# A given TensorE order, fixed loads, longer filler products and a last product by halves in a fused retention and two-product kernel

## The chip, the cores and the metric

The kernel runs on one core of one Trainium2 chip. The metric is the device time of one execution in microseconds (us), lower is better. Times are medians of several executions. Ratios are the mean time of one kernel's fast runs over that of the other's fast runs of the same rounds, so they are not quite the ratios of the medians quoted beside them. A run is called slow if it is over 1.5% above the fastest run of the same kernel. I also group runs by the mean clock that TensorE was granted, which every run records.

## The reference, cut to what matters

```python
# q, k, v: (8, 8, 576, 64) f32;  w_in: (512, 2048);  w_out: (2048, 512)
scores = scale * np.matmul(q, k.transpose(0, 1, 3, 2))
Dmat = np.where(rel >= 0, gamma[:, None, None] ** rel[None, :, :], 0.0)   # decay per head, causal
attn = np.matmul(scores * Dmat[None], v)
x = attn.transpose(0, 2, 1, 3).reshape(4608, 512)
h = x @ w_in              # the "first product"
g = h * np.cos(h)
return g @ w_out          # the "second product"
```

## The kernel before

The attention is done in chunks of 64 tokens, in "sessions" of short 64x64 products (q by k, state, q by state, p by v). They yield x for one of nine blocks of 512 tokens. Each block then goes through the first product (`mlp1`, four matmuls of 512 or, in the early blocks, 256 columns per tile), ACT's sine for the cosine, DVE's multiplication, and the second product. From the second block on, the second product is computed by seven half-size products in place of eight (`wino2`).

The kernel is written as a list of tasks, and a scheduler in Python decides at build time the order of every engine's instructions. Before, that scheduler is greedy. It also keeps an account of TensorE's instructions:

```python
def fetched(t):        # earliest start of task t, by TensorE's instruction count
    k, s = math.ceil(count / 256 - 1.754), 0
    while k >= 0 and (k + 1.754) * 256 <= count + t.ni + (self.MARGIN if t.ni > 60 else 0):
        if k < len(got):
            s = max(s, got[k] - t.dur * ((k + 1.754) * 256 - count) / t.ni)
        elif t.ni > 60:
            s = max(s, free["pe"] + self.FETCH - t.dur)      # FETCH = 6000 ns
        k += 1
    return s
```

`count` is the number of instructions placed so far, a task of many short products (`ni` over 60) isn't started shortly before a border of 256 instructions, and each border assumes that the next one can't be passed within 6 us. I shall call this the guard.

At the start, filler products run on TensorE while data arrives (181 of 128 columns, 14.3 us in all), and the eight slabs of the weight matrices (0.5 MB each, issued from POOL) wait for two events:

```python
inst = e.matmul(ap(self.at(self.wb), 512, 0, 128, 0, [1, 128]), self.ONE.ap(), self.ONE.ap(), ...)   # filler, 128 columns
...
gate = [(self.kv[1, 0, 0]["stgq"],)]                     # q of the second stream
for s, x in enumerate((0, 2, 1, 3)):
    self.load_w("win", x, gate if s >= self.LEAD else [(self.kv[0, 0, 0]["stgv"], 0)], 100 + s)
for s in range(4):
    self.load_w("wout", s, gate, 200 + s)
```

The "second stream" is the second pair of the four sequences of the batch with which the kernel starts; the cast of the second half of its v (`natv`) stands on POOL too.

## Time and profile before

| | before |
|---|---|
| median of the runs before the prediction | 308.38 us (305.6 to 308.73, 3 runs) |
| its profiled run | 312.0 us, span 310.3, clock 0.994, slow |
| TensorE busy | 294.1 us of 310.3 |
| DVE, ACT, POOL busy | 66%, 61%, 35% |

TensorE is the bound and the rest is slack, so the question is where TensorE stands still. The prediction below shows the views that carry this. Two more sets of lines are wanted later for comparison: the queue that brings instructions (packets, MB, share of 16 engines' span), and two windows (columns: stretch, length, then busy us of PE, PEld, which is TensorE's weight loads, DVE, ACT and POOL, each with its number of instructions, then clock, DMA share, GB/s).

```profile
q8 instruction: 34, 0.56, 0.8%
```

### The profile page before, as it was taken

The page shows a single profiled execution, that of the slowest core. Times are in us where ns is not written, and L with a number is a line of the kernel's source. Part 1 is how long each engine was busy: PE and PEld are TensorE (multiplying, and loading weights), DVE is VectorE, ACT ScalarE, POOL GpSimd, SP SyncE. Part 2 cuts the span into 40 slices and gives each one's busy share as a digit, 9 for nine tenths or more (in the row PEclk, how much of TensorE's full clock was granted, in tenths as well). Part 3 has the DMA queues.
Part 4 walks back from the last instruction along what each step waited for, and adds up shares of the span by engine and source line. Part 5 has one row for each costly group of instructions (what it writes and reads, how often), then busy time and mean ns, then how long its engine had stood idle before and what let it go on. Part 6 is the DMA issues. An engine that isn't in the chain of part 4 may idle for free.

```text
span 310.3 us, 10091 instructions
## 1 busy us (share of the span) xinstructions
PE 294.1 (95%) x4274; PEld 214.7 (69%) x4277; DVE 206.3 (66%) x371; ACT 188.3 (61%) x340; POOL 108.9 (35%) x134
## 2 busy tenths in 40 slices
PE   8987999799889999999998799999999999999995
PEld 8866755688778888567855375768656666666684
DVE  3574973475984769898478487775769667666641
ACT  3476843888959775856373566474686665455430
POOL 2261058759517581931362631312741000000000
PEclk9999999999999999999999799999999999999999
DMA  9999999999977999894999749269701100300123
GB/s 172 222 159 206 205 229 217 253 270 219 219 157 189 122 204 285 159 171 109 234 219 247 181 48 235 61 114 195 161 13 72 70 2 0 127 10 2 63 76 136
DMA packets 126397, 46.80 MB, mean 151 GB/s; under 512 B 105104, under 2 KB 122000, under 8 KB 126352
## 3 DMA queue, kind: packets, MB, share of 16 engines
q1 hardware_dynamic: 122128, 41.95, 63.3%
q0 software_dynamic: 4224, 4.19, 8.4%
q8 instruction: 34, 0.56, 0.8%
q14 instruction: 11, 0.09, 0.1%
HBM read 36.70 MB, written 9.44 MB: 149 GB/s over the span
## 4 chain that ended last, share of the span: by engine, by line
PE 87%; DVE 3%; ACT 3%; issue 2%; DMA 2%; POOL 2%; DVEq 0%
PE bk L763 39%; PE bk L886 32%; PE bk L800 4%; PE bk L418 2%; DMA stgq<-in_q_dram 2%; PE bk L661 2%; PE bk L652 2%; PE bk L634 2%; PE st L643 2%; PE bk L575 2%; DVE gt L774 1%; PE bk L593 1%; DVE pt L723 1%; POOL win L743 1%; POOL wout L747 1%
## 5 line engine op out<-in xcount | busy, mean ns | idle before, releaser
L774 DVE TENSOR_TENSOR gt<-bk,cb 128x256 bf16<-128x256 f32 (+1 forms) x192 | 103.7, 555 | 59.5 <-ACT cb L771 52.9
L763 PE MATMUL bk<-xt,win 128*128 128x256 bf16 (+1 forms) x768 | 140.1, 327 | 2.3 <-issue 1.3
L771 ACT ACTIVATE cb<-bk,cpi 128x256 bf16<-128x256 f32 (+1 forms) x192 | 108.4, 585 | 55.6 <-PE bk L763 54.0
L763 PEld LDWEIGHTS bk<-xt,win 128*128 128x128 bf16 x768 | 72.9, 98 | 44.0 <-issue 2.3
L512 POOL TENSOR_TENSOR natv<-stgv,wv 128x512 bf16<-128x512 f32 x38 | 41.3, 1097 | 36.1 <-DMA stgv<-in_v_dram 23.3
L477 POOL CAST natk<-stgk 128x512 bf16<-128x512 f32 x36 | 22.0, 626 | 62.0 <-DMA stgk<-in_k_dram 34.6
L557 POOL TENSOR_TENSOR qnat<-stgq,wq 128x512 bf16<-128x512 f32 x36 | 38.6, 1092 | 13.5 <-DMA stgq<-in_q_dram 5.9
L723 DVE TENSOR_TENSOR pt<-bk,tri 128x512 bf16<-128x512 f32 (+1 forms) x46 | 29.6, 683 | 14.8 <-PE st L643 12.8
L476 ACT ACTIVATE sbd<-st 128x512 bf16<-128x512 f32 x32 | 19.3, 603 | 22.6 <-PE st L643 22.4
L886 PE MATMUL bk<-wout,s 128*128 128x256 bf16 x256 | 32.2, 273 | 0.0
L886 PE MATMUL bk<-tw,s 128*128 128x256 bf16 x256 | 31.6, 273 | 0.5 <-DVE s L847 0.5
L886 PE MATMUL bk<-wout,gt 128*128 128x256 bf16 x256 | 31.6, 273 | 0.0
L886 PEld LDWEIGHTS bk<-wout,s 128*128 128x128 bf16 x256 | 24.7, 98 | 6.6
L886 PEld LDWEIGHTS bk<-tw,s 128*128 128x128 bf16 x256 | 24.6, 98 | 6.1 <-DVE s L847 0.8
L886 PEld LDWEIGHTS bk<-wout,gt 128*128 128x128 bf16 x256 | 24.7, 98 | 4.6 <-DVE pt L723 0.2
L476 ACT ACTIVATE sn<-bk 128x512 f32<-128x512 f32 x24 | 14.4, 604 | 18.7 <-PE bk L886 18.7
L476 ACT ACTIVATE xt<-bk 128x512 bf16<-128x512 f32 x36 | 23.1, 694 | 0.3 <-PE bk L661 0.2
L898 DVE TENSOR_TENSOR os<-bk,sn 128x512 f32<-128x512 f32 x24 | 16.4, 685 | 8.2 <-PE bk L886 8.2
L886 PE MATMUL bk<-tw,gt 128*128 128x256 bf16 x128 | 17.3, 282 | 0.0
L886 PEld LDWEIGHTS bk<-tw,gt 128*128 128x128 bf16 x128 | 12.9, 101 | 4.2 <-issue 0.6
L418 PE MATMUL bk<-one 128*128 128x128 bf16 x181 | 14.3, 244 | 1.1 <-DVE lq L441 1.1
L800 PE MATMUL bk<-wout,gt 128*128 128x512 bf16 x61 | 14.8, 379 | 0.2
(63 smaller groups left out, 230.7 us busy)
## 6 DMA issues: line engine op xcount, KB each, us to landing
stgk<-in_k_dram SPq DMA_DIRECT2D x32, 256.0 KB, 5.0
stgv<-in_v_dram SPq DMA_DIRECT2D x32, 256.0 KB, 5.4
out_dram<-os SPq DMA_DIRECT2D x15, 512.0 KB, 3.5
stgq<-in_q_dram SPq DMA_DIRECT2D x12, 512.0 KB, 7.0
stgq<-in_q_dram SPq DMA_DIRECT2D x8, 256.0 KB, 4.9
win<-in_moe_w_in_dram POOLq DMA_DIRECT2D x4, 512.0 KB, 7.6
wout<-in_moe_w_out_dram POOLq DMA_DIRECT2D x4, 512.0 KB, 14.7
out_dram<-os SPq DMA_DIRECT2D x6, 256.0 KB, 3.5
```

What stands on the lines that cost most here:

```text
L418: inst = e.matmul(ap(self.at(self.wb), 512, 0, 128, 0, [1, 128]), self.ONE.ap(), self.ONE.ap(), start=True, stop=True, skip_group_check=True)
L476: return self.one(eng, dur, lambda e: e.activation(dst(), src(), AF.Copy), r=r, w=w, **kw)
L477: return self.one(eng, dur, lambda e: e.tensor_copy(dst(), src()), r=r, w=w, port=True, **kw)
L512: self.one(ve, vd, lambda e, b2=b2: e.tensor_tensor(ap(self.at(t["natv"]), 1024, 0, 128, 512 * b2, [D, H], [1, D]), ap(self.at(t["stgv"]), ...
L557: self.one("dve" if fast else "pool", 620 if fast else 990, lambda e, t=t, y=y: e.tensor_tensor(ap(self.at(t["qnat"]), 1024, 0, 128, y * 5 ...
L723: self.one("dve", 610, lambda e, hp=hp: e.tensor_tensor(ap(self.at(pt), 1024, p0, n, 512 * hp, [64, 8], [1, 64]), ap(self.at(sc[hp]), 512, ...
L763: inst = e.matmul(ap(self.at(bk), 512, 0, 128, 0, [1, n]), ap(self.WIN, 4 * DFF, 0, 128, c * DFF + 128 * f, [1, 128]), ap(self.at(xt), 204 ...
L771: self.one("act", 70 + n, lambda e: e.activation(ap(self.at(cb), TB, 0, 128, 0, [1, n]), ap(self.at(bk), 512, 0, 128, 0, [1, n]), AF.Sin, ...
L774: self.one("dve", 75 + n / 0.96, lambda e: e.tensor_tensor(ap(self.at(gt), NF * TB, 0, 128, f * TB + 256 * h0, [1, n]), ap(self.at(bk), 51 ...
L800: inst = e.matmul(self.at(bk).ap(), ap(self.at(gt), NF * TB, 0, 128, f * TB + 256 * half + 128 * tt, [1, 128]), ap(self.WOUT, NF * DM, 0, ...
L886: inst = e.matmul(ap(self.at(bank), 512, 0, 128, 256 * tt, [1, 256]), l(f, tt), rr(f), start=(first and f == 0 and tt == 0), stop=True, sk ...
L898: self.one("dve", 610, lambda e: e.tensor_tensor(view(h, c), ap(self.at(bank), 512, 0, 128, 0, [256, 2], [1, 256]), ap(self.at(sn[name]), ...
```

## The change

The intent is to take the last idle time off TensorE: a literal order of TensorE's 412 tasks, found offline, in place of the greedy choice and of the guard; loads in a fixed order; the weight slabs released at three points; fewer and longer filler products; the last product by token halves so that the last copies and stores overlap. The diff also brings a part that its few words don't name: the first product of the last two token blocks by seven products. The core of it, with cuts marked:

```diff
-            deps += [d for d in readers if d.eng != eng or d.sem or sem]
+            deps += [d for d in readers if d.eng != "pe" or eng != "pe"]
...
-        def fetched(t):
-            ... (the guard, and its use when a task is picked)
...
+                if e == "pe" and t.idx != first or e == "sp" and lead and t is not lead[0]:
+                    continue
...
+    SEVEN = 7
+    ORDER = [int(x) for x in """3 2 0 1 9 4 5 7 6 10 8 11 16 20 14 15 12 13 34 21 ... 409 411 410""".split()]
+    FIRST = [(0, "v", 0), (1, "q", 0), (1, "v", 0)]
...
-                inst = e.matmul(ap(self.at(self.wb), 512, 0, 128, 0, [1, 128]), self.ONE.ap(), self.ONE.ap(),
+                inst = e.matmul(self.at(self.wb).ap(), self.ONE.ap(), ap(self.ONE, 128, 0, 128, 0, [0, 4], [1, 128]),
...
+        for s, x in enumerate((0, 2, 1, 3, 4, 5, 6, 7)):
+            x1, n, b2 = self.FIRST[min(s, len(self.FIRST) - 1)]
+            t = self.kv[x1, 0, 0]
+            gate = [(t["stgq", b2],) if n == "q" else (t["stg" + n], b2)]
+            self.load_w("win" if s < 4 else "wout", x % 4, gate, 100 + s)
...
+            if not last and j + 1 >= self.SEVEN:
+                self.xsums(j + 1)
+                for g in range(4):
+                    self.mlp1w(j + 1, g, base + PER * g / 4, PER / 4)      # seven products, 256 columns
...
+                    for f in range(8) if final else range(4 * q, 4 * q + 4):
+                        for tt in (q,) if final else range(2):             # last product: one token half after the other
```

## The prediction

> **What bounds the kernel now.** I read the page first (busy shares and slices), then ten-microsecond windows, then what TensorE waited for, then the chain that ended last.
>
> ```profile
> PE 294.1 (95%) x4274; PEld 214.7 (69%) x4277; DVE 206.3 (66%) x371; ACT 188.3 (61%) x340; POOL 108.9 (35%) x134
> PE   8987999799889999999998799999999999999995
> PEclk9999999999999999999999799999999999999999
> ```
>
> TensorE is the bound: 95% busy, no other engine over 66%. The clock row has one dip, beside a dip of PE. The windows say where the missing 5% lies:
>
> ```profile
> 20.00:30.00 10.00, 6.83 (x139) 5.54 (x140) 6.66 (x14) 6.04 (x13) 4.36 (x6) 1.00 1.20 196
> 50.00:60.00 10.00, 8.12 (x165) 5.19 (x165) 5.48 (x6) 6.00 (x11) 7.61 (x9) 1.00 1.27 241
> 80.00:90.00 10.00, 8.24 (x150) 6.98 (x148) 9.80 (x19) 6.90 (x14) 2.71 (x3) 1.00 1.13 226
> 170.00:180.00 10.00, 7.25 (x67) 4.11 (x68) 4.66 (x7) 5.43 (x9) 6.88 (x7) 0.83 0.64 162
> 250.00:260.00 10.00, 10.00 (x158) 6.90 (x157) 6.58 (x11) 6.13 (x10) 0.00 (x0) 1.00 0.01 2
> 300.00:310.30 10.30, 7.05 (x65) 6.08 (x63) 1.38 (x2) 1.79 (x3) 0.00 (x0) 0.99 0.29 104
> ```
>
> Columns: PE, PEld, DVE, ACT and POOL busy, clock, DMA share, GB/s. Idle PE: 3.2 us in the third window, 1.9, 1.8 and 2.8 in the next three, and 3.2 at the end. The row at 250 is typical of the rest: PE full, everything else with room. Before 20 us PE looks busy but is mostly filler products. What TensorE waited for, then the chain:
>
> ```profile
> PE st L643 <- issue: 3.3, 1, 3.3
> PE bk L634 <- POOL natv L512: 1.8, 1, 1.8
> PE bk L763 <- issue: 1.3, 1, 1.3
> ```
>
> ```profile
> 18.07 2.30 POOL win L743 x3
> 20.36 2.22 POOL wout L747 x3
> 22.59 1.08 POOL natv L512
> ...
> 26.40 2.07 PE bk L763 x18
> 28.47 1.30 issue
> ...
> 165.96 0.86 PE bk L763 x4
> ...
> 169.47 3.28 issue
> ...
> 173.22 1.55 PE bk L763 x4
> ...
> 307.09 0.60 ACT os L476
> ```
>
> Two things to see. The session of the second stream at 23.8 us waited for a cast that stood on POOL behind six weight issues. And twice TensorE stopped for "issue". One L763 tile is four products, so 18 is not a whole number of tiles: no semaphore stands at that place, and the same holds for the other stop, which fell 29 products into a group of 32. I read both as missing instructions. After the second, four 512-column products took 1.55 us instead of 0.86.
>
> [...] Here 8551 PE and PEld instructions make 33.4 blocks, and the instruction queue moved 34 packets of 0.56 MB together[...]. [...] after 3.28 us the rate was 388 ns a product against 215. [...] DMA share is over 1.0 in all windows up to 90 us, at only 160 to 250 GB/s.
>
> **The change part by part.** Most of the diff rewrites the scheduler; what reaches the chip is this.
>
> (a) Not in the change's short title: the first product of the last two token blocks becomes seven products instead of eight (the scheme that the second product has already). One block now costs 64 products of 512 columns, at 0.86/4 = 215 ns: 13.8 us. New: 4 groups x 7 x 4 = 112 products of 256 columns, at 0.87/8 = 109 ns (chain rows of eight): 12.2 us. Gain 1.6 us a block, 3.2 for two, all on TensorE, which is full there. Costs on other engines, per block: ACT +12 copies x 603 ns = 7.2 us; DVE 12 additions x 685 = 8.2 and four sums at some 0.45 us (estimate: half of the 0.78 us row, plus overhead) = 1.8, minus 12 multiplications x 689 = 8.3 that go to POOL, so +1.7; POOL 12 x about 1.1 us (its natv row) = 13.2. Once: eight weight sums on DVE, six at about 0.75 and two in place at 1.49 (the rows of the sums it makes already) = 7.5 us. With PE's 24.4 us a period, ACT comes to 16 x 0.69 + 12 x 0.60 + 2.4 = 20.6 us, DVE to about 21. Both below PE, but at 85%. The accumulating bank is handed to ACT or DVE four times per group; [...] two groups or other products must interleave, as the given order does. I count 2.2 us of the 3.2.
>
> (b) Start. Six of the eight slabs now wait for the second stream's v instead of its q. v was issued from 12.2 to 16.8 us and lands 5 to 6.6 us after each issue starts, so by about 20; its cast began at 22.56. With at most two slabs ahead of it, up to 2.5 us. Fillers shrink from 181 of 128 columns to about 57 of 512 (14.3 us of filler[...]): some 250 instructions, one block, fewer before the stop at 28.5 us, worth up to 1.3. Against it: block 0 has only 13.9 + 13.8 us of products, and the next stream's data is bound by DMA. So of 3.8 I keep 2.
>
> (c) The given order. It interleaves the second batch of sessions with block 0's second product and puts x-side first products between y-side sessions, which should fill most of the 1.9 us at 50 to 60; and it may fill the 1.8 at 80 to 90, where DVE is 98% busy. Keep 2.2 of 3.7.
>
> (d) The long stop: 3.28 idle plus 1.8 at half clock (0.69 for the first four products, 0.84 for the next eight, 0.26 for twelve more) = 5.1 us. It belongs to the profiled run, 312.0 us; the timed runs are 305.6, 308.4 and 308.7, so only part is in their median. Nothing in the new scheduler models instruction fetch, but the order is fixed and probably searched. I count 1.7.
>
> (e) Tail: the last product by token halves lets one half's copy and store leave 0.87 us early, and the last copy covers 256 columns (384 ns in a like row, against 603). About 0.4 us of the 3.2.
>
> Sum: 2.2 + 2.0 + 2.2 + 1.7 + 0.4 = 8.5 us off 308.4, so 299.9. The stricter waits between operations of one engine cost nothing on TensorE, which is exempt. The diff's additional tile in the list without DMA transposes is loaded already with its even neighbour.
>
> **The rivals.** First: the start is DMA's, not the order's. Loads run at 172 to 253 GB/s in the first 60 us; then TensorE finishes block 0 sooner and waits at 50 us. It gives back all of (b), part of (c): about 303. For it: the full DMA row until 90 us. Against: DMA falls to 0.57 at 90 to 100, so buffers also limit it, and x-side work can start on half the data. Second: the seven-product form stalls on its bank handovers or on ACT and DVE at 85%[...]; (a) becomes 0 to -2 us: 302 to 304. For it: three banks a group of six, with sessions in the same period for one of the two blocks. Against: the last block's seven-product second product, alone and on three banks, ran dense (120 products in 13.12 us, 109 each). Third: the fetch stops come back at other places, since sessions spend 256 instructions in about 2 us, and the old scheduler's guard against it is gone: up to 5 us with the half clock, 305. Fourth, upwards: the order removes nearly all idle, including the 5.1 us: 295.
>
> **Range and chances.** Centre 300.0 us (2.7% less). Each rival below takes 2 to 5 us and they can partly add; the upward one gives 5. So 294.5 to 305.5 should hold it 8 times in 10. The 2% line is at 302.2: one rival at half strength still passes, two do not. Faster 0.72, within 2% 0.24, slower 0.04; slower by 6 us would need two fetch stops and a stalled ending.
>
> **What would show it right or wrong.** (a) Two groups of 224 new products at 109 ns; PE at 10.0 per 10 us after 230 us; if it is under 9.7 with waits for ACT or DVE at those products, the second rival holds. (b) The second stream's cast begins by 21 us and the first long run of first products begins before 28; the wait for natv is gone. If PE then waits at 45 to 60 us for a transpose of fresh data, the first rival holds. (c) Windows at 50 to 60 and 80 to 90 above 9.3. (d) No "issue" wait above 1 us and a clock row without a dip. (e) From the last product to the end under 3.0 us. I would be wrong altogether if PE's total idle time did not fall from 16 us to 10 or less.

## More of the kernel before

```profile
60.00:70.00 10.00, 9.71 (x202) 8.25 (x201) 6.64 (x15) 8.13 (x18) 6.35 (x8) 1.00 1.11 269
290.00:300.00 10.00, 10.00 (x84) 8.01 (x82) 6.26 (x10) 3.59 (x6) 0.00 (x0) 1.00 0.28 106
```

The instruction queue moved 34 packets of 16 KB: TensorE's program of 8724 instructions (4277 products of two instructions, a weight load and a matmul, and 170 others) is 34.1 blocks of the guard's 256. The two windows are full: before loses nearly nothing at 60 to 70 us and nothing at 290 to 300.

## The result, and the profile after

| | before | after |
|---|---|---|
| median | 307.61 us (4 runs, 305.6 to 308.73) | 317.24 us (4 runs, 314.4 to 318.74) |
| ratio of fast runs | | 1.031, 95% interval 1.022 to 1.040: slower |
| profiled run | 312.0 us, clock 0.994 | 314.4 us, clock 0.995 |
| TensorE busy, matmuls | 294.1 us, 4274 | 293.3 us, 4239 |
| TensorE idle (span less busy) | 16.2 us | 19.3 us |

The prediction of 300.0 us, with 294.5 to 305.5 as its range, was wrong by 17 us and in sign. After's profile, the page first:

```profile
PE 293.3 (94%) x4239; PEld 214.3 (69%) x4239; DVE 215.6 (69%) x388; ACT 199.7 (64%) x367; POOL 137.2 (44%) x158
...
PE   7978999879999999999995999999999999999796
...
PEclk9999999999999999999999799999999999999999
...
q8 instruction: 33, 0.54, 0.7%
```

The dip of the clock stands at the same place as before, near 172 us (3.41 us at 0.5 in the clock records, from 171.6 us here and from 173.5 in before), and PE has a dip at the end (a 7 ahead of the last 9) that before has not. Products worth 3.2 us were taken away, and ACT, DVE and POOL do more in exchange (64, 69 and 44% busy), but PE's busy time fell by 0.8 us only, and its idle time rose by 3. The windows:

```profile
50.00:60.00 10.00, 9.00 (x192) 6.02 (x190) 5.12 (x7) 6.50 (x13) 8.86 (x10) 1.00 1.23 252
60.00:70.00 10.00, 8.29 (x172) 7.01 (x170) 6.25 (x15) 7.17 (x15) 5.75 (x7) 1.00 1.10 255
...
80.00:90.00 10.00, 9.48 (x159) 7.65 (x158) 8.24 (x16) 8.00 (x17) 6.19 (x7) 1.00 1.15 217
...
170.00:180.00 10.00, 7.98 (x54) 3.93 (x54) 3.39 (x6) 5.83 (x10) 6.50 (x7) 0.83 0.86 208
...
290.00:300.00 10.00, 8.21 (x76) 7.13 (x74) 6.88 (x9) 5.95 (x10) 6.03 (x5) 1.00 0.29 106
```

The windows at 50 and 80 us are fuller than before (9.00 against 8.12, 9.48 against 8.24), as predicted, though only the second passes the 9.3 that the prediction asked for. But 60 to 70 lost 1.4 us that before did not lose, 170 to 180 is as bad as before, and 290 to 300 lost 1.8. What TensorE waited for (in total, times, longest):

```profile
PE bk L702 <- issue: 4.1, 3, 2.9
PE bk L929 <- ACT stgv L517: 2.1, 2, 1.8
...
PE bk L804 <- issue: 1.5, 1, 1.5
...
PE bk L804 <- DMA win<-in_moe_w_in_dram: 1.3, 1, 1.3
...
PE bk L675 <- POOL natv L553: 0.5, 1, 0.5
```

"issue" is a wait for nothing that the profile shows: 5.6 us of it. L929 is the new seven-product first product, waiting for a copy on ACT. The wait for a weight slab (1.3 us, from 20.3 us on) is new. The chain at the start and around the stops:

```profile
12.56 9.83 DMA stgv<-in_v_dram
22.39 0.07 issue
22.47 1.05 POOL natv L553
...
67.93 0.11 PE bk L804
68.04 1.53 issue
69.58 0.49 PE bk L804 x3
...
169.03 0.10 PE bk L702 x11
169.13 2.89 issue
172.02 0.48 PE bk L702 x12
172.50 3.97 PE bk L804 x12
...
294.70 0.58 ACT stgv L517
...
299.00 10.73 PE bk L1062 x96
```

The cast of the second stream's v, which was to come by 21 us, begins at 22.47, as late as in before (22.59 in its chain): there it stood behind the slabs on POOL, here it waits for v itself, whose transfer took 9.8 us. At 68.04 TensorE stops after one of the four products of a tile; at 169.13 after 11 products of a session. No semaphore stands there. And the twelve 512-column products after the long stop took 3.97 us against 12 x 0.215 = 2.59 at full rate.

**Where the time went.** To compare two programs of different work I took, at each point of time, the time passed less the full-rate time of all products started by then, fillers not counted. This "lost time" is worked out from the trace's matmul records; before is its profiled run.

```text
lost by (us)     30     60     70     90    110    130    180    230    300    end
before         22.0   26.5   28.6   32.0   33.6   35.6   41.9   43.0   45.9   49.4
after          21.6   24.7   28.1   30.9   33.9   35.5   41.6   44.0   50.9   54.2
```

Three of before's matmul records are missing (61 of L800 for 64 weight loads, at 35 to 54 us), so from 60 us on its row is some 0.6 us too high. With that taken off, after is 1.2 us ahead at 60 and 0.9 behind by 110, and it loses 4.0 us more than before from 230 to 300, where the seven-product form saved 3.2 us of products. This profile of after is its fastest run of four, and that of before is among its slow ones; so the profiles show less than the medians do. Repeating the two, and the runs' clocks, fill that in.

### The profile page after: what moved, and what is told of

Read it like the earlier page. It is cut to its first block, busy times and chain, and to the rows that moved or that the text cites.

```text
span 312.6 us, 10068 instructions
## 1 busy us (share of the span) xinstructions
PE 293.3 (94%) x4239; PEld 214.3 (69%) x4239; DVE 215.6 (69%) x388; ACT 199.7 (64%) x367; POOL 137.2 (44%) x158
## 4 chain that ended last, share of the span: by engine, by line
PE 79%; DMA 5%; DVE 4%; ACT 4%; issue 4%; SPq 2%; POOL 1%; DVEq 0%; POOLq 0%; ACTq 0%
PE bk L804 30%; PE bk L1062 29%; PE bk L929 7%; DMA stgv<-in_v_dram 5%; PE bk L974 4%; PE bk L675 2%; PE bk L693 2%; PE bk L702 2%; PE st L684 1%; PE bk L616 1%; SPq L591 1%; PE bk L634 1%; ACT sbd L517 1%; DVE s L1027 1%; DVE gt L815 1%
## 5 line engine op out<-in xcount | busy, mean ns | idle before, releaser
L815 DVE TENSOR_TENSOR gt<-bk,cb 128x256 bf16<-128x256 f32 (+1 forms) x160 | 82.0, 529 | 50.8 <-ACT cb L812 47.3
L804 PE MATMUL bk<-xt,win 128*128 128x256 bf16 (+1 forms) x640 | 107.3, 318 | 4.7 <-ACT xt L517 1.7
L812 ACT ACTIVATE cb<-bk,cpi 128x256 bf16<-128x256 f32 (+1 forms) x160 | 85.3, 560 | 31.2 <-PE bk L804 29.7
L804 PEld LDWEIGHTS bk<-xt,win 128*128 128x128 bf16 x640 | 61.0, 98 | 37.5 <-issue 3.6
L518 POOL CAST natk<-stgk 128x512 bf16<-128x512 f32 x36 | 22.2, 631 | 76.3 <-PE st L684 41.0
L912 POOL TENSOR_TENSOR gt<-stgv,cb 128x512 bf16<-128x512 f32 x16 | 19.5, 1223 | 29.3 <-ACT cb L908 28.6
L517 ACT ACTIVATE sbd<-st 128x512 bf16<-128x512 f32 x32 | 19.3, 602 | 20.5 <-PE st L684 20.4
L517 ACT ACTIVATE sn<-bk 128x512 f32<-128x512 f32 (+1 forms) x26 | 14.5, 571 | 11.7 <-PE bk L1062 11.4
L1081 DVE TENSOR_TENSOR os<-bk,sn 128x512 f32<-128x512 f32 (+1 forms) x25 | 16.6, 664 | 7.6 <-PE bk L1062 6.8
L1062 PE MATMUL bk<-tw,gt 128*128 128x256 bf16 x128 | 16.5, 273 | 0.0
L908 ACT ACTIVATE cb<-stgv,cpi 128x512 bf16<-128x512 f32 x16 | 11.4, 720 | 7.4 <-DVE stgv L919 7.2
L517 ACT ACTIVATE os<-bk 128x512 f32<-128x512 f32 (+1 forms) x13 | 7.4, 566 | 13.6 <-PE bk L1062 8.6
```

Source lines behind the costliest of these rows:

```text
L517: return self.one(eng, dur, lambda e: e.activation(dst(), src(), AF.Copy), r=r, w=w, **kw)
L518: return self.one(eng, dur, lambda e: e.tensor_copy(dst(), src()), r=r, w=w, port=True, **kw)
L804: inst = e.matmul(ap(self.at(bk), 512, 0, 128, 0, [1, n]), ap(self.WIN, 4 * DFF, 0, 128, c * DFF + 128 * f, [1, 128]), ap(self.at(xt), 204 ...
L812: self.one("act", 70 + n, lambda e: e.activation(ap(self.at(cb), TB, 0, 128, 0, [1, n]), ap(self.at(bk), 512, 0, 128, 0, [1, n]), AF.Sin, ...
L815: self.one("dve", 75 + n / 0.96, lambda e: e.tensor_tensor(ap(self.at(gt), NF * TB, 0, 128, f * TB + 256 * h0, [1, n]), ap(self.at(bk), 51 ...
L912: self.one(eng, 608 if eng == "dve" else 1120, lambda e: e.tensor_tensor(out(h, n), ap(self.at(buf), size, 0, 128, 512 * o, [256, 2], [1, ...
```

## The experiments

"old_" is the kernel before with one thing altered, "new_" is the kernel after. All gave correct results. Some expectations name theories A and B; each text says what it means.

### 1. Both kernels again

No edit.

> The kernel before, unchanged, for a profile in the fast state (the one at hand was a slow run, 312.0 us) and as a check of the comparison itself. All theories: 306 to 309 us, ratio 1.00. Fetch theory: since the slow profile lost 5.1 us to one stop of 3.3 us for instructions and the half clock after it, a run near 306 should show no stop for issue above 1.5 us and no dip in the clock row.

> The changed kernel, unchanged, for a second profile. Its profiled run was the fastest of four (314.4; the others 317 to 319). Fetch theory: a run of 317 us shows one or two more stops for issue, or longer ones, than the profile at hand (1.5, 0.6, 2.9 and 0.6 us), and its ending from 230 us on is the same. Ending theory: the additional 3 us lie after 230 us, in waits for ACT or DVE at the new products.

Measured: old_again 310.46 us (305.34 to 313.17); new_again 319.69, ratio 1.041 [1.028, 1.054]. The loss is there in another session too, and larger. new_again's profile (span 316.6) has the stop at 68 us and one that after's profile lacks:

```profile
PE bk L702 <- issue: 3.2, 2, 2.6
...
PE bk L616 <- issue: 1.9, 1, 1.9
PE bk L804 <- issue: 1.8, 1, 1.8
```

```profile
90.95 4.26 PE bk L1062 x24
```

The stop of 1.9 us at 87.9 us is followed by 24 products of 256 columns in 4.26 us, against 24 x 0.109 = 2.6. So the same program stops at different places from run to run, and after this stop of 1.9 us the products came at 178 ns each in place of 109.

The clock sorts the runs. Over all rounds, all runs of the kernel before (with old_again) and all of after (with new_again):

```text
mean clock of the run     before: runs, mean us     after: runs, mean us
0.998 and above           20     307.5              0
0.992 to 0.995            10     310.6              2     315.9
0.986 to 0.989             7     311.6              2     317.9
below 0.986                7     314.1              4     320.3
all                       44     309.9              8     318.6
```

The profiles of before (mean 0.994) and of after (0.995) have one stretch at half clock each, of 3.41 us, and with one such stretch the mean is 0.993 to 0.995 in every profile that I read. By its mean clock before has runs without one in 20 of 44 cases; after never. Of the difference of the means, 8.7 us, 5.3 is there at an equal clock (315.9 less 310.6), and 3.4 is after having more such stretches. (With two runs in a cell the split is rough.)

Not every such stretch follows a stop for instructions. The clock row of new_again has three dips, the first at 26 us:

```profile
PEclk9997999999979999999999799999999999999999
```

From 14 to 30 us TensorE waited there for a slab (1.4 us), for x (0.7), for natv (0.6) and twice more (0.7), and for no instruction. The profiles of new_no_seven, new_plus138 and old_order_all have a dip in the same slice, also without an issue stop before it. That makes four of the nine profiles with the change's loads and fillers or most of them; of the nine with before's own fillers none has it. So in some runs a part of after's lower clock comes from its start.

### 2. Where TensorE stops

Walking TensorE's program (two instructions a product, one for an extra semaphore wait) and marking where it stood at each issue stop gives this:

```text
kernel            stops, as instruction index / 256 (us of stop)
before            3.758 (1.3)   20.758 (3.3)
after             6.762 (1.5)   11.758 (0.6)   19.762 (2.9)   26.762 (0.6)
new_again         6.762 (1.8)    8.762 (1.9)   19.762 (2.6)   26.762 (0.6)
```

Each stop has the same fraction of a block, 0.76, at whatever work stands there. The packets of the instruction queue fit. In the profiles of before and after there are 34 and 33 of them, as many as such borders; in 55 of these 67 cases the packet starts after TensorE passed the border, it takes 0.9 to 1.45 us, and TensorE resumes from the six stops 1.2 to 1.6 us after it landed (in all 19 profiles up to 2.0 and 1.8). Over all 19 profiles the start comes 0.3 us after the border on average where no transfer is in flight (160 borders; some packets there start up to 2.7 us ahead of it) and 2.3 with three to five in flight (361 borders), up to 8.6; in before and after alone it is 0.3 over 17 borders and 2.4 over 38. From these figures I estimate the least time between two borders without a stop at the second: some 3 us with nothing in flight (0.3, 1.2 for the packet, 1.4 to resume), up to 11 at worst (with 8.6 in place of 0.3). Blocks of that order occur: the shortest (stops taken out) of before are 4.7, 5.0 and 5.1 us, those of after 2.6 (at 101 us), about 4 (at 64) and 4.6 (at 211).

That gives a test: shift the borders without touching the work. A filler of 512 columns cut into four of 128 takes nearly the same time (216 ns in after's trace, 4 x 56 in before's; 427 until 4.4 us and 4 x 107 until 6.2) and adds six instructions; joining two takes two away.

```diff
 # new_plus48 and new_plus138: the first CUT = 8 or 23 fillers cut into four
+                cut = 4 if self.CUT > 0 else 1
+                self.CUT -= 1
+                for c in range(cut):
+                    inst = e.matmul(..., [1, 512 // cut] ...)
 # old_minus112: 56 pairs of fillers joined into one of 256 columns
+                two = 2 if self.MERGE > 0 and n > 1 else 1
 # old_no_guard: the guard switched off
         def fetched(t):
+            return 0
```

> The changed kernel with eight of its start fillers cut into four products of 128 columns each: 24 more products, so 48 more TensorE instructions ahead of everything else, in the same time; order, data and waits unchanged. Fetch theory: every stop for issue so far ended at an instruction index of a whole number of blocks of 256 plus 0.758 (3.758, 6.762, 8.762, 11.758, 19.762, 20.758, 26.762), so instructions arrive in blocks[...]. Moving the borders by 48 raises the shortest blocks from 2.6, 3.9, 4.6, 4.7 us to 4.3, 4.7, 4.7, 5.3 us [...]. So: 3 to 8 us faster than the changed kernel, 311 to 315 beside 308 for before. All other theories (ending, loads, waits of one engine, fillers as such): no change, 317 to 320.

> The same with 23 fillers cut into four: 69 more products, 138 more instructions. [...] Fetch theory: clearly slower than the changed kernel, 325 to 340, with more stops for issue and more half clock in the profile, each at a block index ending in about .76. All other theories: no change, 317 to 320.

> The kernel before with 112 of its fillers joined two by two into products of 256 columns: 56 products, 112 instructions fewer at the start, same time, all else unchanged. Fetch theory: its scheduler placed the work for the block borders it had; [...] it becomes as slow as the changed kernel or slower, 318 to 335. All other theories: no change, 306 to 310.

> The kernel before with the scheduler's account of instruction blocks switched off (it then never delays or swaps a session for the next block), as the change does; the rest of its scheduler stays. Fetch theory: new stops for issue appear, slower by 3 to 12 us, 311 to 320. If the guard is of no use: 306 to 310.

Measured, with before at 307.23:

```text
new_plus48      314.07 us (312.35 to 314.7)     ratio 1.023 [1.018, 1.028]
new_plus138     316.97 us (315.45 to 321.77)    ratio 1.030 [1.025, 1.036]
old_minus112    311.59 us (311.4 to 314.93)     ratio 1.017 [1.010, 1.024]
old_no_guard    318.62 us (318.59 to 318.92)    ratio 1.037 [1.034, 1.041]
```

The stops moved to the new borders: new_plus138 at 5.758, 13.758 (3.0 us), 18.762 and 25.758; old_minus112 at 1.762 (2.6), 13.762, 20.758 and 21.762. The shift that looked good helped, by 3 us against after's 317.24 (another session, so roughly), but my two bad shifts were far less bad than expected: 317 in place of 325 or more, 311.6 in place of 318 or more. The 325 and the 318 rested on an estimate of mine of how long a block must last, which is not shown. The lengths of the blocks alone don't foretell the cost: before runs through blocks of 4.7 and 5.0 us without a stop, and in after the block of 2.6 us led to a stop of 0.6, one of 4.7 us to the stop of 2.9. The strongest result is old_no_guard, all of whose runs agree within 0.4 us: the kernel before, with the guard off, is as slow as the changed kernel.

```profile
PE bk L662 <- issue: 3.9, 2, 2.9
PE bk L764 <- issue: 3.7, 3, 1.6
...
PE st L644 <- issue: 0.9, 1, 0.9
```

That is 8.5 us of stops, at six borders (3.758, 9.766, 10.758 with 2.9 us, 11.758, 13.762, 20.758), where before has 4.6 at two. Between the two profiles (spans 316.9 and 310.3 us, one stretch at half clock in each) the stops make 3.9 of the 6.6 us. Switching the guard off also changes the greedy order, so the 11 us are the guard's whole worth, its order included, and not stops alone.

### 3. The seven-product first product

```diff
 # old_seven: before with win_sums, xsums and mlp1w of the change for the last two blocks, and its stricter waits
+            if not last and j + 1 >= self.SEVEN: ...
-            deps += [d for d in readers if d.eng != eng or d.sem or sem]
+            deps += [d for d in readers if d.eng != "pe" or eng != "pe"]
 # new_no_seven, new_plus48_no_seven: the change (and its plus48) with eight products; the given order mapped, 28 places to 16
-    SEVEN = 7
+    SEVEN = 99
```

Without the stricter waits the check finds a race in old_seven, so those waits belong to this part.

> The kernel before with the seven-product first product of the last two blocks alone (its own scheduler places the new products; the stricter waits between operations of one engine come with it, since the check finds a race without them). Ending theory: slower than before by 1 to 4 us, 309 to 312. If the form itself is sound and only the rest of the change is bad: faster by 1 to 3 us, 305 to 307.

> The changed kernel with the first product of the last two blocks put back to eight products (its 28 places in the given order taken by 16 whole tiles); all else as changed. Ending theory (the seven-product form costs more than it saves: 3.2 us of products saved, but from 230 us to the end 3.9 us more lost than before): faster than the changed kernel by 1 to 4 us, 313 to 316, and no wait for ACT copies in the last 80 us. Fetch theory (the loss is the stops for instructions before 230 us): about 3 us slower than the changed kernel, since the saving goes: 319 to 321. Mixed: unchanged.

> The changed kernel with the 48 additional filler instructions (314.1 us) and with the first product of the last two blocks at eight. Ending theory in its weak form (the form is neutral: 3.2 us saved, as much given back in waits and drains after 230 us): 313 to 316, no wait for ACT copies near 295 us. If the seven-product ending carries what is left of the loss (6.8 us over before): 308 to 311.

Measured: old_seven 308.98, ratio 1.0017 [0.992, 1.011]. new_no_seven 322.04 beside new_again's 319.69 on the same chip (all but one of its runs slow, no ratio). new_plus48_no_seven 314.0, 1.018 [1.002, 1.034], beside new_plus48's 314.07. So no gain is shown on either base, though the form takes 3.2 us of products away. A small one isn't excluded: old_seven's interval reaches down to 2.4 us less than before, and at an equal clock (below 0.986) new_no_seven's three runs average 322.5 us against 320.3 of new_again's four. After's trace has part of the reason at the ending: the wait for the ACT copy at 295 us (1.8 us, and 0.35 at 277): the 1.8 us stand in every profile of the new order with seven products and in none with eight. That shows where 2.1 us go; the rest of the 3.2 I have not traced.

### 4. The old scheduler on the changed kernel

```diff
 # old_order_rest: the class Graph of before (greedy order, guard) and its PERIOD, T0, T1 in the kernel after,
 # with eight products
-        self.G.run(self.ORDER)
+        self.G.run(None)
 # old_order_all: the same with seven products
```

> The changed kernel with the scheduler of the kernel before put back (its own TensorE order, its account of instruction blocks, counted with the new fillers), and the first product of the last blocks at eight: what is left of the change are the weight slabs released at three points, the 512-column fillers and the last product by token halves. Fetch-and-order theory (the loss comes with the given order, which lacks the account of blocks): as fast as before or a little faster, 304 to 309. If the loads, fillers or ending by halves are to blame: 311 or more.

> The same with the seven-product first product of the last two blocks: the whole change but for the order (and its model). Fetch-and-order theory: 304 to 310, some 8 to 12 us faster than the changed kernel, the only difference being which product stands where. If the seven-product form is to blame by itself: 2 us or more over the run without it.

Measured: old_order_rest 313.9, ratio 1.018 [1.008, 1.028]; old_order_all 313.53, 1.014 [0.998, 1.029]; before 310.96 there. This refuted my belief that order and guard were all of it: I had expected 304 to 310. The trace of old_order_rest is 2 us ahead of before at 70 us and then loses some 7.5 more than before in 70 to 110, mostly in waits for DVE (over the whole run three for a multiplication, 3.1 us, and two for sums, 2.4) and one stop at border 12.762. One of its runs has a clock of 1.0 and still took 313.2. So either the new release of the slabs costs, or the greedy order, run again on other inputs, came out badly.

### 5. Slabs alone, tail alone, and the change without its slabs

```diff
 # old_slabs_late: before with every order pinned; only the four wout slabs move behind the cast of the second
 # stream's v on POOL, and wait for that v
+        late = [t for t in order if slab(t)][self.KEEP:]          # KEEP = 4
+        for t in late:
+            t.parts[0][2][:] = [v]
+        order = [t for t in order if t not in late]
+        i = order.index(cast) + 1
+        return order[:i] + late + order[i:]
 # old_first: before with FIRST and its loop from the change; the greedy scheduler runs again
 # old_tail: before with wino2's last product, its copies and stores from the change
 # new_old_gates: the change with the slabs' gates of before
```

> The kernel before with TensorE's, ACT's, DVE's and SP's order untouched; only the four slabs of the second weight matrix move on POOL from ahead of the cast of the second stream's v to behind it, and wait for that v. Theory A (the loss of the kernel with the old scheduler on the new loads and fillers came from the order its re-run produced and from where the fetch borders fell): this one is at 305 to 309 us, equal to before or up to 1.5 us faster, and the wait of TensorE for natv (1.8 us) shrinks below 0.5 us. Theory B (the new release of the slabs itself costs[...]): 311 to 314 us, with DMA's loads landing later in 20 to 60 us.

> The kernel before with the three release points of the change for the slabs, and its greedy scheduler run again on that; fillers and tail as before. Theory A: its order changes in 40 to 80 us and so do the fetch borders, so anything from 304 to 312 us, and where it is slow the trace shows issue stops or waits for DVE between 60 and 110 us. Theory B: 311 to 315 us, about as the kernel with the new loads and fillers (313.9), with late landings.

> The kernel before with only the last product by token halves and its stores by halves; TensorE's order and instruction count nearly the same. By the prediction's step for the tail 0.3 to 0.5 us less than before: 0.998 to 0.999 of it, and from the last product to the end under 2.95 us. The rival: the added copies and stores give it back, ratio 1.000 to 1.002.

> The changed kernel with its given TensorE order, its 512-column fillers and everything else, but the slabs released as before (one, then seven on the second stream's q); 12 more fillers of 512 columns come in, 24 instructions. Theory A: the given order loses as before, 315 to 320 us. Theory B: 310 to 313 us, since the released slabs were the cause.

Measured, before at 309.6:

```text
old_slabs_late   307.13 us (304.56 to 311.03)   ratio 0.998 [0.982, 1.014]
old_first        309.22 us (308.57 to 310.65)   ratio 1.006 [0.997, 1.015]
old_tail         312.33 us (308.18 to 312.62)   ratio 1.012 [1.000, 1.024]
new_old_gates    321.67 us (319.12 to 322.05)   ratio 1.044 [1.034, 1.054]
```

This speaks for theory A: the release of the slabs isn't what costs most. Alone it doesn't slow the kernel before by anything that shows (its interval leaves room for 1.5%), and taking it out of the changed kernel leaves that slow, with issue stops of 8.3 us at the borders 6.762, 8.758, 9.758 and 19.758. But the late landings that theory B speaks of are there. In all nine profiles with the three release points the second slab is issued at 14 to 15 us, and the second half of the second stream's v lands at 22.2 to 22.9 us; in the ten others, new_old_gates among them, that slab goes out at 17 us or later and v lands at 19.8 to 20.3.

old_tail shows a trap of the fast and slow labels. Its fastest run is 308.18, so its runs of 312 count as fast; before's fastest is 305.38, so before's runs from 309.98 on count as slow. At equal clock it is 308.2 (one run) against 307.5, and 312.4 against 310.6: no gain. Yet in its trace the end came as predicted: from the last product to the end 2.82 us, against 3.23 before. 0.4 us are below what these runs resolve.

### 6. The same kernel twice, with and without a stop

> The same kernel as old_slabs_late, timed in five rounds, since its first interval (0.982 to 1.014) left open whether it beats the kernel before. Theory A2: its 2 us of lead at 60 us hold to the end and it has fewer fetch stops; ratio 0.988 to 0.996, median about 305 to 307, more of its runs at a mean clock of 0.998 or more than of before. Rival: the stops at 170 us come and go by chance in both, ratio 0.997 to 1.003.

> As old_slabs_late, but the fourth slab of the first weight matrix moves behind the cast as well, so five slabs wait for the second stream's v. Theory A2: the session of the second stream starts another 0.2 to 0.5 us earlier, but the first products of block 0 may wait for the slab; ratio to before 0.988 to 1.000. Rival: the late slab stops TensorE at the first products for 1 us or more, ratio 1.000 to 1.006.

old_slabs_three has `KEEP = 3`: one slab more behind the cast. Measured: old_slabs_again 308.82, ratio 1.0035 [0.996, 1.011]; old_slabs_three 310.4, 1.0018 [0.993, 1.011]; before 311.45 there. No version beats the kernel before by more than the noise (at a clock of 0.998 and above the five runs of old_slabs_late and old_slabs_again average 306.4 us, those of before 307.5, from 305.3 to 311.4). But old_slabs_late and old_slabs_again are one kernel, and one was profiled at 302.8 us of span, the other at 308.1. The first:

```profile
PE   8899999899999999999999999999999999999995
PEclk9999999999999999999999999999999999999999
```

```profile
165.94 0.38 PE bk L665 x32
166.32 0.27 PE bk L647 x30
166.58 0.29 PE st L656 x32
166.87 0.27 PE bk L674 x31
167.14 0.97 PE bk L776 x4
168.11 0.87 PE bk L899 x8
168.98 2.59 PE bk L776 x12
```

The second, at the same place of the same program:

```profile
167.12 0.38 PE bk L665 x32
167.50 0.27 PE bk L647 x30
167.76 0.27 PE st L656 x29
168.03 2.46 issue
170.49 0.22 PE st L656 x3
170.71 0.25 PE bk L674 x30
170.95 1.07 PE bk L776 x4
172.03 1.71 PE bk L899 x8
173.73 3.34 PE bk L776 x12
```

The first runs through the session and on at full rate. The second stops three products short of the end of a group, and then eight 256-column products take 1.71 us in place of 0.87 and twelve of 512 columns 3.34 in place of 2.59. From 160 to 180 us the lost time grows by 0.7 in the first and by 4.8 in the second: 4.1 of the 5.3 us between the two spans. (Another stop, of 1.2 us at 84, is part of the rest.) The packets of the instruction queue differ:

```text
border 19.758 to 20.758          before   old_tail   old_slabs_late   old_slabs_again
next packet started after (us)     7.09       6.78             2.60              6.54
it took                            1.15       1.21             1.51              0.91
landed until TensorE resumed       1.41       1.39         no stop              1.39
stop                                3.3        3.0                0               2.5
```

The same border, the same instructions; only the start of the packet differs, by 4 us. Why it does is not shown: the transfers around it are nearly the same in all four traces. The start of the kernel shows the same thing: in old_slabs_late the packet after border 2.758 started at 3.18 us, in before at 6.44, and the 1.3 us stop at 3.758 is gone in one and not in the other.

## Why the prediction was wrong, point by point

The prediction took 8.5 us off; the medians say 9.6 us on.

**(d), the long stop, is the step that failed.** The prediction took 1.7 us off with the words "Nothing in the new scheduler models instruction fetch, but the order is fixed and probably searched." It saw the mechanism, named the missing guard, and then reckoned that a search had replaced it. It had not: after's profile has stops of 5.6 us at four borders (68, 104, 169 and 236 us) where before's has 4.6 at two, none of the eight runs of after is, by its mean clock, free of a half-clock stretch against 20 of 44 of before, and before without its guard is as slow as after (318.62). The third rival was right in kind ("the fetch stops come back at other places"), but I gave it 5 us and 305; by old_no_guard the guard, with the order that it makes, is worth 11 us. There was also little to win: the median of 308.4, from which the prediction started, is already close to the 307.5 of before's runs without a half-clock stretch. And I counted stops in one profile, though they vary from run to run.

How much of the loss these stops explain is only partly shown. Shifting the borders (new_plus48) gave back some 3 of the 9.6 us; it stayed 6.8 us over before in its own session. At an equal clock it brings the runs with one half-clock stretch from after's 315.9 to 312.35, before's standing at 310.6. So at an equal clock some 3.5 of the 5.3 us would be borders, and 1.8 not (one run against two that lie 3 us apart, so this is rough). What makes up those 1.8, and the 5.7 us by which the one run of old_order_rest at a clock of 1.0 (313.2) stays behind before's 307.5, was shown only so far as that waits for DVE and ACT lie there. Whether the longer fillers, the order's choices or the loads cause them stays open: the release points, the tail and the stricter waits were run alone (old_first, old_tail, within old_seven) and cost nothing that shows, the longer fillers and the fixed order of loads were not.

**(a), 2.2 us from the seven-product form: not found.** Counting 2.2 of the 3.2 was an estimate. By old_seven and the run with eight products on the shifted borders it is near neutral, though a gain of some 2 us isn't excluded. The second rival holds at its mild end (0 of -2 to 0). The prediction's own test was "if it is under 9.7 with waits for ACT or DVE at those products"; the window at 290 to 300 has 8.21, with such a wait. The counterargument, that the second product runs dense on three banks, fails because there the operands are all there beforehand, whereas here the ending waits for copies and multiplications that the new form itself adds (1.8 us for one copy at 295 us).

**(b), 2.0 us from the start: failed in the changed kernel.** The prediction had v land "by about 20" whatever else was released, and the cast begin by 21. But with the second slab released at 14 us, in flight beside it, v's second half landed at 22.39 us (19.86 in before; experiment 5 has all profiles), the cast began at 22.47 (22.56), and TensorE stood 1.3 us for a slab instead. The wait for natv fell from 1.8 to 0.5 us because TensorE came to it later, not because the cast came sooner; from 20 to 30 us TensorE is busy for 6.97 us, against 6.83. (The first long run of first products did begin before 28, at 26.88, since the stop for instructions at 28 is gone.) So the first rival, that the start is DMA's, is right in kind for these first 30 us; at 45 to 60 us, where it was to show itself, it isn't: PE was at 9.00 in 50 to 60 us, with a DMA share of 1.23 against 1.27. The idea itself works where the slabs are moved behind the cast and none is released early: in old_slabs_late v landed at 20.27, the cast began at 20.36, and the trace is 2.0 us ahead from 30 us on and keeps that to 160. Yet ten runs of that kernel don't beat before: one stop at 170 us, which some runs have and some not, is worth twice that.

**(c), 2.2 us from the order: two windows fuller, paid back.** The windows at 50 and 80 us did fill, by 0.9 and 1.2 us (to 9.00 and 9.48; above 9.3 was asked for), and the one at 60 lost 1.4 that before did not, with a fetch stop of 1.5 in it. I had judged the windows one by one, without asking what would stand at the borders afterwards.

**(e), 0.4 us from the tail: right in the trace** (2.86 us from the last product to the end, "under 3.0" predicted; 2.82 in old_tail), not resolved in time.

**The sum.** It assumed that each idle piece, once filled, stays filled. "I would be wrong altogether if PE's total idle time did not fall from 16 us to 10 or less": it rose to 19. Chances of 0.04 for "slower" rested on "two fetch stops and a stalled ending" being rare together. After's profile has both: two long stops (1.5 and 2.9 us) and a wait of 1.8 us at the ending. Smaller slips changed nothing: the fillers are 47 and not 57, the shortest block of after takes 2.6 us and of before 4.7 where "about 2 us" was reckoned, and the windows up to 90 us read 182 to 269 GB/s and not 160 to 250.

## What to carry to other kernels

If a tuned kernel's scheduler contains an odd rule with a fitted constant (here 256 and 0.754), find out what it answers before counting on a change that drops it; switching it off alone is the first experiment to make (here 318.62 us against 307.23). For a TensorE-bound kernel with runs of very short products, check every stop that is called "issue" against the instruction count: if they share one fraction of 256 (here 0.76), the program's layout is part of the schedule, and an edit that adds or removes instructions early moves the later stops (with 138 more they stood at 5.76, 13.76, 18.76 and 25.76 blocks here, in place of 6.76, 11.76, 19.76 and 26.76). When a load is released earlier, look also at when the others land (here v at 22.39 us in place of 19.86). And sort runs by granted clock before comparing: a kernel that has two kinds of runs will otherwise hide or fake a per cent (old_tail: ratio 1.012 by the labels, and at an equal clock 308.2 us against 307.5 and 312.4 against 310.6).

## What these traces show of the stops and of the clock

- TensorE stopped at the borders for 0.6 us (after) to 3.8 us (old_again) at a time, up to 8.5 us in a profile (old_no_guard), and in one profile not at all (old_slabs_late).
- Stops of 1.5 us (new_no_seven, at 89 us), 1.9 us (new_again), 2.5 us (old_slabs_again), 2.9 us (after) and 3.3 us (before) were each followed by a stretch at half rate, 3.41 us long in the clock records of before and after, while the stop of 1.5 us in after (at 68) was not. With the half clock the stops of 1.9, 2.5 and 3.3 us cost 1.5 to 1.9 times their length.
